# The last chunk's output projection in three PSUM banks (256, 256, 128 columns), stored as 512 and 128 columns

## Chip, cores, metric

The kernel runs on one core of a Trainium2 chip. The metric is the device time of one execution in microseconds (us); of repeated runs the median is quoted. "The profile" is one profiled execution; its span is the time from its first to its last instruction, here about 1.3 us shorter than the run's own time. Words used below: a bank is a piece of PSUM (`PS` in the code), the memory into which TensorE writes its sums; taking a bank out of it is an eviction; a store is issued by an instruction of a queue and lands when its completion is signalled; the tail is what follows TensorE's last matmul. In the profile's lines PE is TensorE, PEld its weight loads, DVE VectorE, ACT ScalarE, SPq and ACTq the queues of SyncE and ScalarE.

## The reference, cut to what matters

```python
g = sigmoid((x * gate_w).sum(-1, keepdims=True))
a = 2.0 * einsum("blp,dp->bld", hseq, Cmat).real + x * Dskip   # state space branch, hseq: a scan over L
b = gelu(x @ w1 + b1) @ w2 + b2                                # dense branch
return g * a + (1 - g) * b                                     # 2048 x 640, bfloat16
```

There are 2048 rows of 640 columns, taken as 16 chunks of 128 rows. What is changed is the last step of the last chunk: the product of the scanned state with `Cmat` (real and imaginary part, 5 blocks of 128 each, so 10 matmuls for each block of columns), times the gate, plus everything else.

## The kernel before

For every chunk `c`, `cproj(c)` multiplies the state `H` by `CT` into two PSUM banks. For all chunks but the last, ScalarE takes the banks out into `E2`, VectorE adds the three parts in two steps, and one store writes 128 x 640. For the last chunk the sum of the other parts is made ahead in `E2`, VectorE takes each bank out with one instruction (times gate, plus `E2`), and each part is stored as soon as it is there:

```python
CCOLS = (slice(0, D - 256), slice(D - 256, D))          # 384 and 256 columns

def cproj(c):
    for hf in range(2):
        bank = next_bank()
        cbank[hf] = bank
        cols = CCOLS[hf] if c == NCH - 1 else slice(hf * HALF, (hf + 1) * HALF)
        n = cols.stop - cols.start
        def f_mm(bank=bank, cols=cols, n=n):
            for ci in range(2):
                for k in range(KP):       # KP = 5
                    t = nc.tensor.matmul(PS[bank][:, 0:n], H[b % NHB][:, ci, k, s * 128:(s + 1) * 128],
                                         CT[:, ci, k, cols], start=(i == 0), stop=(i == 2 * KP - 1))
        # ... other chunks: ScalarE evicts to E2
def comb(c):
    # ...
    if c == NCH - 1:
        # "last": E2 = xg + E1
        for hf in range(2):
            cols = CCOLS[hf]
            def f_fin(...):   # VectorE: osb[:, cols] = PS * gcol + E2[:, cols]
            def f_st(...):    # SyncE:  o2[c * 128:(c + 1) * 128, cols] <- osb[:, cols]
        return
```

## Time and profile before

| | before |
|---|---|
| median of 3 runs | 213.53 us (213.41 to 214.03) |
| span of the profiled run | 212.3 us |
| TensorE busy | 99% |
| from TensorE's last matmul to the end of the span | 2.1 us |

First the page of the kernel before: the busy time of each engine (with its share and its number of instructions), and the chain of work that ended last.

```profile
PE 209.3 (99%) x1264; PEld 120.6 (57%) x1264; DVE 189.2 (89%) x262; ACT 111.3 (52%) x201; POOL 3.0 (1%) x11
...
PE 99%; DVE 0%; issue 0%
```

The chain is TensorE's from one end to the other. Its last pieces in order of time (start, length, what; kernel before):

```profile
204.69 5.45 PE ps L817 x40
210.13 0.03 issue
210.16 0.48 DVE osb L850
```

Line 817 is the projection; the 40 matmuls are those of the last two chunks. After them come one eviction and a store. The timeline of VectorE at the end (start, length, engine, line, operation, tiles; in brackets the idle time before it and what ended that):

```profile
208.00 0.49 DVE L480 TENSOR_TENSOR osb<-xg,E 128x640 bf16<-128x640 bf16 x1 [2.15 <-ACT E L828]
208.53 0.49 DVE L480 TENSOR_TENSOR osb<-osb,E 128x640 bf16<-128x640 bf16 x1
209.07 0.62 DVE L850 SCALAR_TENSOR_TENSOR osb<-ps,gcol,E 128x384 bf16<-128x384 f32 x1
210.16 0.48 DVE L850 SCALAR_TENSOR_TENSOR osb<-ps,gcol,E 128x256 bf16<-128x256 f32 x1 [0.47 <-PE ps L817]
```

VectorE is not the bound here: it sits idle for 0.47 us before the last eviction, until TensorE has filled the bank. The queue of SyncE, and the transfers by size with their median time from issue to landing:

```profile
209.04 0.33 SPq L870 DMA_DIRECT2D out_dram<-osb  x1
209.71 0.33 SPq L856 DMA_DIRECT2D out_dram<-osb  x1
210.67 0.33 SPq L856 DMA_DIRECT2D out_dram<-osb  x1
```

```profile
out_dram<-osb SPq DMA_DIRECT2D x1, 96.0 KB, 1.6
out_dram<-osb SPq DMA_DIRECT2D x1, 64.0 KB, 1.5
```

So what follows TensorE is 0.48 us of eviction and about 1.6 us of store. Apart from the ten matmuls that it adds, the change can act on nothing else.

### The profile page before, as it was taken

The page shows a single profiled execution, that of the slowest core. Times are in us where ns is not written, and L with a number is a line of the kernel's source. Part 1 is how long each engine was busy: PE and PEld are TensorE (multiplying, and loading weights), DVE is VectorE, ACT ScalarE, POOL GpSimd, SP SyncE. Part 2 cuts the span into 40 slices and gives each one's busy share as a digit, 9 for nine tenths or more (in the row PEclk, how much of TensorE's full clock was granted, in tenths as well). Part 3 has the DMA queues.
Part 4 walks back from the last instruction along what each step waited for, and adds up shares of the span by engine and source line. Part 5 has one row for each costly group of instructions (what it writes and reads, how often), then busy time and mean ns, then how long its engine had stood idle before and what let it go on. Part 6 is the DMA issues. An engine that isn't in the chain of part 4 may idle for free.

```text
span 212.3 us, 3122 instructions
## 1 busy us (share of the span) xinstructions
PE 209.3 (99%) x1264; PEld 120.6 (57%) x1264; DVE 189.2 (89%) x262; ACT 111.3 (52%) x201; POOL 3.0 (1%) x11
## 2 busy tenths in 40 slices
PE   8999999999999999999999999999999999999995
PEld 3444444444567776444466777444446777767773
DVE  2499999999999999999999969899999999899443
ACT  2489556678905234556953233556792444722330
POOL 2000000000000010000000001000000000000000
DMA  5999799997000004100000014000000000010011
GB/s 147 316 263 203 161 221 317 274 213 173 24 0 3 31 31 127 62 0 0 0 3 0 0 36 154 31 31 3 0 0 2 3 31 31 31 34 0 31 34 62
DMA packets 31318, 16.35 MB, mean 77 GB/s; under 512 B 22984, under 2 KB 30408, under 8 KB 31304
## 3 DMA queue, kind: packets, MB, share of 16 engines
q1 hardware_dynamic: 30928, 14.83, 27.4%
q0 software_dynamic: 320, 1.31, 2.0%
q8 instruction: 10, 0.16, 0.3%
q14 instruction: 4, 0.03, 0.1%
q10 hardware_dynamic: 56, 0.01, 0.0%
HBM read 7.63 MB, written 2.62 MB: 48 GB/s over the span
## 4 chain that ended last, share of the span: by engine, by line
PE 99%; DVE 0%; issue 0%
PE ps L769 27%; PE ps L639 22%; PE ps L817 20%; PE ps L682 20%; PE ps L619 4%; PE ps L399 1%; PE ps L783 1%; PE ps L660 1%; PE ps L411 0%; DVE osb L850 0%; PE ps L430 0%
## 5 line engine op out<-in xcount | busy, mean ns | idle before, releaser
L769 PE MATMUL ps<-W2sb,Gl 128*128 128x320 bf16 x416 | 59.2, 299 | 0.0
L769 PEld LDWEIGHTS ps<-W2sb,Gl 128*128 128x128 bf16 x416 | 40.4, 98 | 17.0 <-issue 1.1
L639 PE MATMUL ps<-xT,W1sb 128*128 128x512 bf16 x220 | 48.1, 379 | 0.0
L817 PE MATMUL ps<-CT,H 128*128 128x320 bf16 (+2 forms) x320 | 45.4, 299 | 0.0
L722 DVE TENSOR_TENSOR_SCAN W<-atab,V 128x1280 bf16<-128x1280 f32 x16 | 44.3, 2811 | 0.3
L682 PE MATMUL ps<-xT,BT 128*128 128x512 bf16 x200 | 43.8, 379 | 0.0
L817 PEld LDWEIGHTS ps<-CT,H 128*128 128x128 bf16 x320 | 31.3, 98 | 12.2
L797 ACT ACTIVATE E<-ps,g1col 128x320 bf16<-128x320 f32 x32 | 16.3, 527 | 39.7 <-PE ps L769 25.5
L639 PEld LDWEIGHTS ps<-xT,W1sb 128*128 128x128 bf16 x220 | 21.6, 98 | 25.9
L646 ACT ACTIVATE Gl<-ps,cols 128x512 bf16<-128x512 f32 x44 | 29.6, 689 | 10.0 <-PE ps L639 10.0
L682 PEld LDWEIGHTS ps<-xT,BT 128*128 128x128 bf16 x200 | 19.4, 98 | 23.5 <-ACT Gt L668 0.4
L691 ACT ACTIVATE U<-ps 128x512 bf16<-128x512 f32 x40 | 23.8, 597 | 14.9 <-PE ps L682 14.9
L828 ACT ACTIVATE E<-ps,gcol 128x320 bf16<-128x320 f32 x30 | 15.8, 527 | 22.6 <-PE ps L817 22.6
L756 ACT ACTIVATE ps<-b2b 128x320 f32<-128x320 bf16 x32 | 14.1, 442 | 1.1
L480 DVE TENSOR_TENSOR osb<-xg,E 128x640 bf16<-128x640 bf16 x15 | 7.3, 488 | 7.9 <-ACT E L828 7.5
L836 DVE SCALAR_TENSOR_TENSOR xg<-xn,gcol,dsk 128x640 bf16<-128x640 bf16 x16 | 13.9, 883 | 0.4
L596 DVE SCALAR_TENSOR_TENSOR scr<-xn,gwb 128x640 bf16<-128x640 bf16 x16 | 13.2, 823 | 0.4
L480 DVE TENSOR_TENSOR V<-V,W 128x1280 bf16<-128x1280 bf16 x16 | 12.5, 821 | 0.3
L480 DVE TENSOR_TENSOR H<-H,V 128x1280 bf16<-128x1280 bf16 x16 | 12.5, 821 | 0.3
L480 DVE TENSOR_TENSOR V<-mr,U 128x2560 bf16<-128x2560 bf16 x8 | 11.9, 1489 | 0.2
L480 DVE TENSOR_TENSOR H<-c,W 128x2560 bf16<-128x2560 bf16 x8 | 11.9, 1490 | 0.2
L480 DVE TENSOR_TENSOR V<-s,W 128x2560 bf16<-128x2560 bf16 x8 | 11.9, 1484 | 0.0
(80 smaller groups left out, 100.2 us busy)
## 6 DMA issues: line engine op xcount, KB each, us to landing
out_dram<-osb SPq DMA_DIRECT2D x15, 160.0 KB, 1.8
W2sb<-in_B_w_dram SPq DMA_DIRECT2D x1, 2080.0 KB, 9.2
W1sb<-in_B_w_dram SPq DMA_DIRECT2D x5, 256.0 KB, 4.8
xn<-in_A_x_dram POOLq DMA_DIRECT2D x2, 640.0 KB, 4.7
xn<-in_A_x_dram SPq DMA_DIRECT2D x1, 640.0 KB, 7.7
W1sb<-in_B_w_dram SPq DMA_DIRECT2D x1, 480.0 KB, 5.8
W1sb<-in_B_w_dram SPq DMA_DIRECT2D x1, 400.0 KB, 6.4
xn<-in_A_x_dram SPq DMA_DIRECT2D x1, 384.0 KB, 6.0
```

Of the source, the lines that this page charges most:

```text
L480: return inc("dve", nc.vector.tensor_tensor(out=o, in0=a, in1=b, op=o_))
L639: t = nc.tensor.matmul(PS[bank][:, :], W1sb[:, k, jf * 128:(jf + 1) * 128], xT[q][:, k, :], start=(k == 0), stop=(k == KD - 1))
L646: return inc("act", nc.scalar.activation(Gl[q % 2][:, jf, :], PS[bank][:, :], ACT.Gelu_apprx_tanh, bias=b1col[:, jf:jf + 1]))
L682: t = nc.tensor.matmul(PS[bank][:, :], BT[:, ci, kd, k * 128:(k + 1) * 128], xT[q][:, kd, :], start=(kd == 0), stop=(kd == KD - 1))
L691: return inc("act", nc.scalar.activation(dst, src, ACT.Copy, scale=1.0 if ci == 0 else -1.0))
L722: t = inc("dve", nc.vector.tensor_tensor_scan(out=g[:, ci, :], data0=a, data1=v[:, ci, :], initial=0.0, op0=ALU.mult, op1=ALU.add))
L756: return inc("act", nc.scalar.activation(PS[bank][:, 0:HALF], b2b[:, cols], ACT.Copy))
L769: t = nc.tensor.matmul(PS[bank][:, 0:HALF], Gl[q % 2][:, jf, t4 * 128:(t4 + 1) * 128], W2sb[:, jf, cols], start=False, stop=False, skip_gr ...
L797: return inc("act", nc.scalar.activation(E1[c % NE][:, cols], PS[bank][:, 0:HALF], ACT.Copy, scale=g1col[:, c:c + 1]))
L817: t = nc.tensor.matmul(PS[bank][:, 0:n], H[b % NHB][:, ci, k, s * 128:(s + 1) * 128], CT[:, ci, k, cols], start=(i == 0), stop=(i == 2 * K ...
L828: return inc("act", nc.scalar.activation(E2[c % NE][:, cols], PS[bank][:, 0:HALF], ACT.Copy, scale=gcol[:, c:c + 1]))
L836: return inc("dve", nc.vector.scalar_tensor_tensor(out=xg[c % 2][:, :], in0=xn[q % 2][:, c % 4, :], scalar=gcol[:, c:c + 1], in1=dsk[:, :] ...
```

## The change

The intent: what is done after the last matmul should be smaller. The last bank gets 128 columns in place of 256, so that its eviction and its store are shorter. The other 512 columns are cut in two banks, so that VectorE can take out the first while TensorE fills the second; both go out in one store. The price is ten more matmuls with their weight loads, one more eviction, and rows of 256 bytes in the last store. The cut-down diff:

```diff
-        CCOLS = (slice(0, D - 256), slice(D - 256, D))
+        CCOLS = (slice(0, 256), slice(256, D - 128), slice(D - 128, D))
+        SCOLS = (slice(0, D - 128), slice(D - 128, D))
 
         def cproj(c):
-            for hf in range(2):
+            for hf in range(len(CCOLS) if c == NCH - 1 else 2):
 ...
-                for hf in range(2):
-                    cols = CCOLS[hf]
+                for hf, cols in enumerate(CCOLS):
 ... one eviction (fin) for each bank, marking ("osbl", hf); it waits for the store of chunk c - NO, as before
+                for i, cols in enumerate(SCOLS):
+                    def f_st(i=i, cols=cols):
+                        return dma_inc("sp", nc.sync.dma_start(o2[c * 128:(c + 1) * 128, cols], osb[c % NO][:, cols]), f"stl{i}")
+                    op(f"stl{i}", "sp", 0.5, [("osbl", hf) for hf in ((0, 1), (2,))[i]], [], f_st, prio=1000 + c, lat=2.5)
```

More of the change, by code (lines that the diff above doesn't have):

```diff
@@ L830, in cproj @@
                 op(f"e2_{c}_{hf}", "act", d_act(HALF), [("bank", bank), ("g", q)], [("E2", c % NE, hf)], f_ev, prio=5)
+        stores = {}
         def comb(c):
@@ L851, in f_fin @@
                                                                         in1=E2[c % NE][:, cols], op0=ALU.mult, op1=ALU.add))
-                    op(f"fin{hf}", "dve", d_dve(HALF), [("bank", cbank[hf]), ("E2", c % NE, 0), ("E2", c % NE, 1)], [("osb", c % NO, hf)], f_fin, prio=-60)
-                    def f_st(hf=hf, cols=cols):
-                        return dma_inc("sp", nc.sync.dma_start(o2[c * 128:(c + 1) * 128, cols], osb[c % NO][:, cols]), f"stl{hf}")
-                    op(f"stl{hf}", "sp", 0.5, [("osb", c % NO, hf)], [], f_st, prio=1000 + c, lat=2.5)
+                    op(f"fin{hf}", "dve", d_dve(cols.stop - cols.start), [("bank", cbank[hf]), ("E2", c % NE, 0), ("E2", c % NE, 1)], [("osbl", hf)], f_fin,
+                       prio=-60, after=[stores[c - NO]])
+                for i, cols in enumerate(SCOLS):
+                    def f_st(i=i, cols=cols):
+                        return dma_inc("sp", nc.sync.dma_start(o2[c * 128:(c + 1) * 128, cols], osb[c % NO][:, cols]), f"stl{i}")
+                    op(f"stl{i}", "sp", 0.5, [("osbl", hf) for hf in ((0, 1), (2,))[i]], [], f_st, prio=1000 + c, lat=2.5)
                 return
@@ L870, in f_st @@
                 return dma_inc("sp", nc.sync.dma_start(o2[c * 128:(c + 1) * 128, :], osb[c % NO][:, :]), f"st{c % NO}")
-            op(f"st{c}", "sp", 0.5, [("osb", c % NO, 0), ("osb", c % NO, 1)], [], f_st, prio=1000 + c, lat=2.5)
+            stores[c] = op(f"st{c}", "sp", 0.5, [("osb", c % NO, 0), ("osb", c % NO, 1)], [], f_st, prio=1000 + c, lat=2.5)
         def outs(q, mid=None):
```

## The prediction

> **What bounds the kernel now.** The engine table gives TensorE 209.3 of 212.3 us (99%), VectorE 189.2, and the chain of waits is 99% TensorE. The change touches only what follows the last matmuls. The timeline of the last microseconds shows: the last chunk's projection starts at about 207.26; its 384-column bank needs 10 matmuls at about 163 ns, its 256-column bank 10 at about 109 ns. VectorE finishes chunk 14's combine at 209.02, evicts 384 columns at 209.07 (0.62 us), then idles 0.47 us for TensorE, and evicts 256 columns at 210.16 (0.48 us, to 210.64). The queue issues the stores at 209.71 and 210.67 (0.33 us of sequencer each); the tables of transfers give issue to landing 1.6 us (96 KB) and 1.5 us (64 KB). So the tail after the last matmul is 0.04 + 0.48 + 0.03 + 1.5 + about 0.1 = 2.2 us, 1% of the span. Nothing else can move.
>
> **What changes.** The projected columns stay 640. Ten matmul/weight-load pairs are added: 20 pairs become 30 (256, 256, 128 columns). One eviction is added, and the last becomes 128 columns. Two stores remain: 128 KB and 32 KB (256-byte rows instead of 512).
>
> - Matmuls: the trace's pace fits columns/2400 + 2.5 ns (136 ns at 320). If that holds at 128 columns (56 ns), TensorE ends about 0.02 us later. The Trainium skill, "TensorE: Matmul & The Clock Gate", section "Back-to-back issue gap", gives about 81 ns for a sustained weight-load/matmul stream at 128 columns; then it ends 0.27 us later. No warm 128-column stream is in this trace; the eight cold transposes at the start go at about 105 ns, equal to 128 columns at half clock, so loads hid there. I lean towards 60 to 75 ns: 0.05 to 0.2 us later. The last matmul itself drains 0.05 us sooner (219 ns against 272 for one of 256).
> - Evictions: two PSUM sizes give 1.05 ns per column (618 and 484), so 128 columns cost about 0.35 us (estimate), 0.13 less. VectorE: first 256 at 209.06 to 209.54; second when its bank is done, 209.63 to 210.11; the 128 can start at 210.15 at the earliest and, by TensorE, at 210.20 (56 ns) to 210.43 (81 ns). It ends at 210.55 to 210.78, before: 210.64.
> - Stores: the 128 KB store issues at about 210.14, landing about 1.7 us later (211.85), not last. The sequencer is free at 210.47. The 32 KB store issues at 210.58 to 210.81, before 210.67. Data start about 0.85 us after issue, when the 128 KB (about 0.5 us of movement) has just finished, so little collision. Landing falls only slightly from 1.5: 96 to 64 KB saved just 0.1 us. Risk: the skill's "DMA: Bandwidth & Descriptors", "Specifications", says that below 512 bytes the engine does a read-modify-write; no store in this trace shows it.
>
> All of it is on the critical path: eviction -0.13, drain -0.05, weight loads +0.02 to +0.27, landing -0.1 to +0.1. Sum about -0.25 to +0.2, centre -0.05 us.
>
> **Prediction:** 213.45 us, 8 in 10 within 213.1 to 213.85. Faster by over 2%: 0.5%; within 2%: 99%; slower: 0.5%.
>
> **What would show each step.** Timeline at the end: ten 128-column matmuls 56 to 81 ns apart; the last eviction about 0.35 us, starting 210.2 to 210.4; the larger store issued near 210.14, the smaller near 210.7; table of transfers: 32 KB landing 1.4 to 1.5 us. TensorE's start of the projection and everything earlier unchanged to 0.1 us.
>
> **What would make it wrong.** Weight loads at 98 ns each not hidden (+0.4 us); 256-byte rows landing slower; the two stores, now 0.5 us apart rather than 0.96, queueing on the same engines; a changed instruction order before the last chunk. Run-to-run spread (213.41 to 214.03) exceeds the effect.

## The result, and the profile after

| | before | after |
|---|---|---|
| median of 6 runs each | 213.47 us (213.16 to 214.03) | 213.49 us (213.26 to 213.88) |
| ratio | | 0.9999, 95% interval 0.9982 to 1.0015 |
| span of the profiled run | 212.3 us | 212.0 us |

A ratio here is the mean time of one kernel's fast runs over the mean of the other's of the same rounds, so it is not quite the ratio of the medians. The result is "the same". But the interval is 0.33% wide, 0.7 us, and the whole tail is 2.1 us. Whether the change did anything can only be seen in the trace. The lines of the kernel after that answer to those above, first the page:

```profile
PE 208.5 (98%) x1264; PEld 121.1 (57%) x1274; DVE 189.3 (89%) x263; ACT 111.3 (53%) x201; POOL 3.0 (1%) x11
...
PE 96%; DMA 2%; SPq 0%; issue 0%; DVE 0%
```

There are ten more weight loads and one more VectorE instruction. (There must be ten more matmuls too: ten matmul records of earlier stages, lines 619, 639 and 682, are missing from this trace.) The "DMA 2%" in the chain lies in the loading phase at the start, of which more below. The chain's last pieces, VectorE's timeline and the queue of the kernel after:

```profile
204.60 5.47 PE ps L818 x50
210.07 0.03 issue
210.10 0.35 DVE osb L852
```

```profile
208.85 0.48 DVE L852 SCALAR_TENSOR_TENSOR osb<-ps,gcol,E 128x256 bf16<-128x256 f32 x1
209.54 0.49 DVE L852 SCALAR_TENSOR_TENSOR osb<-ps,gcol,E 128x256 bf16<-128x256 f32 x1 [0.21 <-PE ps L818]
210.10 0.35 DVE L852 SCALAR_TENSOR_TENSOR osb<-ps,gcol,E 128x128 bf16<-128x128 f32 x1
```

```profile
210.05 0.33 SPq L861 DMA_DIRECT2D out_dram<-osb  x1
210.47 0.39 SPq L861 DMA_DIRECT2D out_dram<-osb  x1
```

```profile
out_dram<-osb SPq DMA_DIRECT2D x1, 128.0 KB, 1.7
out_dram<-osb SPq DMA_DIRECT2D x1, 32.0 KB, 1.5
```

Two traces must be lined up before such small times are compared: the two kernels reached the last projection at different moments (204.69 and 204.60 in the chain) though nothing before it was changed. So from here on, times count **from the first matmul of the last chunk's projection**, and are taken from the trace's records at 1 ns:

| us from the projection's start | before | after | difference |
|---|---|---|---|
| TensorE's last matmul ends | 2.881 | 2.905 | +0.024 |
| last eviction starts | 2.919 | 2.944 | |
| last eviction takes | 0.484 | 0.349 | -0.135 |
| last store's issue starts | 3.431 | 3.321 | |
| last store's issue takes | 0.332 | 0.387 | +0.055 |
| its first data move, after the issue's end | 0.501 | 0.513 | +0.012 |
| its data take | 0.348 | 0.265 | -0.083 |
| last data to end of span | 0.399 | 0.401 | +0.002 |
| **end of span** | **5.011** | **4.887** | **-0.124** |

The terms add up to the difference (within 1 ns of rounding). The matmuls and the narrower eviction behave as wanted. In the store, most of the 0.08 us that fewer bytes save is given back by a longer issue. That was to be explained.

### The profile page after: what moved, and what is told of

Same layout as the page of the kernel before. It is cut to its first block, busy times and chain, and to the rows that moved or that the text cites. A ratio compares the mean times of both kernels' runs of the same rounds, so it can differ in the third digit from the quotient of the medians.

```text
span 212.0 us, 3133 instructions
## 1 busy us (share of the span) xinstructions
PE 208.5 (98%) x1264; PEld 121.1 (57%) x1274; DVE 189.3 (89%) x263; ACT 111.3 (53%) x201; POOL 3.0 (1%) x11
## 4 chain that ended last, share of the span: by engine, by line
PE 96%; DMA 2%; SPq 0%; issue 0%; DVE 0%
PE ps L769 27%; PE ps L639 22%; PE ps L818 21%; PE ps L682 20%; PE ps L619 3%; DMA W1sb<-in_B_w_dram 2%; PE ps L783 1%; PE ps L660 1%; SPq L326 0%; DVE osb L852 0%; PE ps L430 0%
## 5 line engine op out<-in xcount | busy, mean ns | idle before, releaser
L639 PE MATMUL ps<-xT,W1sb 128*128 128x512 bf16 x215 | 47.5, 379 | 0.3
L682 PE MATMUL ps<-xT,BT 128*128 128x512 bf16 x196 | 43.1, 379 | 0.3 <-issue 0.2
L818 PEld LDWEIGHTS ps<-CT,H 128*128 128x128 bf16 x330 | 32.0, 98 | 11.7
```

The lines of the kernel that those rows point to most:

```text
L639: t = nc.tensor.matmul(PS[bank][:, :], W1sb[:, k, jf * 128:(jf + 1) * 128], xT[q][:, k, :], start=(k == 0), stop=(k == KD - 1))
L682: t = nc.tensor.matmul(PS[bank][:, :], BT[:, ci, kd, k * 128:(k + 1) * 128], xT[q][:, kd, :], start=(kd == 0), stop=(kd == KD - 1))
```

## The experiments

The theory: the change shortens the tail by a real 0.12 us, which is 0.06% and less than the noise of a run. The rivals: the difference of the traces is chance; only the narrow last eviction counts and the third bank is not needed; the split of the stores counts for nothing; or the 256-byte rows or the collision of the two stores eat up a larger gain. Each kernel below was timed in 5 rounds but for the last two, and all gave correct results. The edits are against the kernel after, unless said otherwise.

### 1. The kernel before, against itself

> The kernel before against itself: the noise of the comparison and the repeatability of the tail. All theories: same time, ratio 1.000 within its interval of about +-0.0015. In the profile: from the first matmul of the last chunk's projection to the end of the span 5.01 us within 0.03 (5.011 in the first trace), whatever the span does; from the start of the last store's issue to the end 1.58 us. If the first number scatters by more than 0.1 us, the 0.12 us that the first pair of traces shows for the change proves nothing.

Measured: the end comes 5.006 us after the projection's start (5.011 in the first trace), the last issue 1.576 us before the end. The time was 213.58 us against 213.72, ratio 0.9994, interval 0.9983 to 1.0006. So the tail repeats to 5 ns, while the timing of a kernel against itself is off by 0.06%, just the size that is sought.

### 2. The kernel after, again

> The changed kernel again. Theory 'small real gain, drowned': from the first matmul of the last projection to the end 4.89 us within 0.03 (4.887 in the first trace; before 5.011), and a measured ratio between 0.998 and 1.001, centred near 0.9994. Rival 'no gain at all, the first traces differed by chance': 5.0 us in the tail as before.

Measured: 4.879 us (4.887 in the first trace). The gain of 0.12 to 0.13 us in the tail is no chance. The time: 213.41 us against 213.72, ratio 0.9992, interval 0.9980 to 1.0003. This is no resolved gain either.

Where does the noise come from? The chain of waits in the first 20 us shows where it arises. These are single lines of the kernel before, of the kernel after, of the second run of the kernel after, and of the kernel of experiment 8 (`old_tail`):

```profile
14.09 5.40 PE ps L639 x25
```

```profile
14.00 5.40 PE ps L639 x25
```

```profile
14.64 5.39 PE ps L639 x25
```

```profile
13.74 5.40 PE ps L639 x25
```

Line 639 is the first layer's second part, the first matmuls after the load phase. Their start scatters by 0.9 us over these four traces. The last projection starts at 207.240, 207.154, 207.788 and 206.895 us in the same four: 193.15 us later each time, within 0.01 us. (The records at 1 ns say the same of all 13 traces of this document: from the first record of line 639 to the projection 193.315 to 193.318 us.) So nearly all of the scatter before the tail arises in the first 14 us. There the chain changes hands from run to run: in the second run of after it goes through the load of `xn`, in the first through a load of `W1sb`, in before through TensorE alone.

```profile
0.75 3.06 DMA xn<-in_A_x_dram
...
8.38 4.75 PE ps L619 x22
```

```profile
1.80 4.59 DMA W1sb<-in_B_w_dram
...
8.65 3.84 PE ps L619 x17
```

(The first fence is of the second run of after, the second of the first.)

The change of hands is not the cause by itself: in the second run of before the chain goes through `xn` too, and line 639 starts at 14.10 us, as in the first. The records of line 619, the matmuls before those of line 639, show what differs. They start 216 ns apart, but in some traces the first of them start about 427 ns apart, half the pace: before has two such slow steps, the second run of after four, the first run of after none. That second run starts line 639 0.55 us later than before does; of this, 0.10 us is a later start of line 619 (4.84 against 4.74 us) and 0.44 us the longer slow stretch. The first run of after instead loses 0.23 and 0.20 us in two stops of TensorE between these matmuls. Why the slow stretch is longer in one run than in another was not tested.

### 3. Two banks of 512 and 128: the store split alone

```diff
-CCOLS = (slice(0, 256), slice(256, D - 128), slice(D - 128, D))
+CCOLS = (slice(0, D - 128), slice(D - 128, D))
-((0, 1), (2,))[i]
+((0,), (1,))[i]
```

> The store split alone, with two banks of 512 and 128 columns. Theory: VectorE becomes the bound of the tail. The 512-column bank completes 2.36 us after the projection's start, its eviction takes about 0.75 us (estimate: 0.484 at 256 columns plus 1.05 ns for each further column), so the 128-column eviction starts at about 3.14 us after TensorE has been done 0.2 us, and the end comes 5.08 us after the projection's start: 0.2 us later than the changed kernel and 0.07 later than the kernel before. Rival 'only the width of the last eviction and the size of the last store count': 4.89 us, as the changed kernel.

Measured: the end at 5.12 us, 0.24 later than the kernel after and 0.11 later than the kernel before. (One matmul record of this projection is missing; the start was fixed by ScalarE's last eviction before it, which follows the start by 0.201 to 0.202 us in the other traces.) The time was 213.78 us, ratio 1.0004, interval 0.9991 to 1.0016. The rival is refuted by the tail: with 512 columns in the first bank, the third bank is needed. VectorE and the queue of this kernel:

```profile
209.51 0.75 DVE L852 SCALAR_TENSOR_TENSOR osb<-ps,gcol,E 128x512 bf16<-128x512 f32 x1 [0.58 <-PE ps L818]
210.18 0.34 DVE L852 SCALAR_TENSOR_TENSOR osb<-ps,gcol,E 128x128 bf16<-128x128 f32 x1
```

```profile
210.29 0.33 SPq L861 DMA_DIRECT2D out_dram<-osb  x1
210.66 0.43 SPq L861 DMA_DIRECT2D out_dram<-osb  x1
```

The 128-column eviction starts as soon as the 512-column one lets it, as the theory said, even 0.08 us before the other's recorded end (so it is done earlier than expected). But then the store queue holds it: the first issue is still running when the last eviction ends at 210.52, and the second takes 0.43 us. That part was not in the theory.

### 4. Three banks, one store of 640 columns

```diff
-SCOLS = (slice(0, D - 128), slice(D - 128, D))
+SCOLS = (slice(0, D),)
```

> Three banks as changed, but one store of 640 columns after the last eviction. Evictions unchanged: the last ends 3.29 us after the projection's start. Theory 'a store's landing grows with its bytes': 160 KB take 0.26 us longer to the last byte than 32 KB (1.42 against 1.17 us from issue in the traces so far), so the end comes at 5.14 us, and the gain of the change is lost twice over. Rival 'landing is a fixed cost and the split of the stores does nothing': 4.89 us.

Measured: the last eviction ends at 3.293 us, its store is issued at once, in 0.332 us, and the end comes at 5.141 us, where 5.14 was expected. The time was 213.71 us, ratio 0.9996, interval 0.9983 to 1.0009. The bytes of the last store count: without the split of the stores the three banks are worse than the kernel before.

### 5. One store for each bank

```diff
-SCOLS = (slice(0, D - 128), slice(D - 128, D))
+SCOLS = CCOLS                                       # 64, 64, 32 KB
-((0, 1), (2,))[i]
+((0,), (1,), (2,))[i]
```

> The changed kernel with one store per bank (64, 64, 32 KB). The last 32 KB store then follows 64 KB in place of 128 KB on the same engines. Theory 'the 32 KB store is a little delayed by the 128 KB store before it' (its data begin 0.90 us after issue, against 0.83 for the last store of the kernel before): data begin at 0.83 to 0.85 us and the end comes at 4.82 to 4.85 us after the projection's start. Rival 'the sequencer or descriptor generation is what delays it, by the number of stores': the end is at 4.89 us or later, and the issue of the last store takes 0.36 us or more again.

Measured: the end at 4.863 us, 0.02 earlier than after and between the two theories (4.82 to 4.85, and 4.89 or later). The last issue takes 0.385 us again, and its first data follow the issue's end by 0.498 us (0.505 and 0.513 in the two traces of after). So the collision with the 128 KB costs 0.01 to 0.02 us, and the stretch of the issue does not depend on the bytes of the store before it: it was another cause. The time was 213.40 us, ratio 0.9990, interval 0.9977 to 1.0002.

### 6. A last bank of 64 columns

```diff
-CCOLS = (slice(0, 256), slice(256, D - 128), slice(D - 128, D))
-SCOLS = (slice(0, D - 128), slice(D - 128, D))
+CCOLS = (slice(0, 256), slice(256, D - 64), slice(D - 64, D))
+SCOLS = (slice(0, D - 64), slice(D - 64, D))
```

> Banks of 256, 320 and 64 columns, stores of 576 and 64 columns. Rival 'the narrower the last eviction the better': 0.28 us in place of 0.35, end at 4.82 us after the projection's start. Theory 'VectorE queues': the 320-column bank completes at 2.66 us, its eviction takes 0.55 us to 3.21, the 64-column one ends at 3.51 and the end comes at about 5.08 us, 0.2 later than the changed kernel. And the pace of ten 64-column matmuls: 29 ns if columns/2400 + 2.5 ns still holds, about 56 ns if a weight load of 128 columns sets the floor.

Measured: the end at 5.182 us, 0.30 later than after. The time was 213.67 us, ratio 1.0009, interval 0.9995 to 1.0022. The evictions and the queue:

```profile
209.70 0.55 DVE L852 SCALAR_TENSOR_TENSOR osb<-ps,gcol,E 128x320 bf16<-128x320 f32 x1 [0.48 <-PE ps L818]
210.16 0.27 DVE L852 SCALAR_TENSOR_TENSOR osb<-ps,gcol,E 128x64 bf16<-128x64 f32 x1
```

```profile
210.27 0.33 SPq L861 DMA_DIRECT2D out_dram<-osb  x1
210.65 0.43 SPq L861 DMA_DIRECT2D out_dram<-osb  x1
```

The rival is refuted: a narrower last eviction made the tail longer. VectorE is again late with the middle bank, though by less than the theory said: the last eviction ends 3.39 us after the projection's start, where 3.51 was expected and where the kernel after has 3.29. The rest is added by the store queue: the last eviction ends at 210.44, but its store's issue starts at 210.65, behind the other, and takes 0.43 us.

The ten 64-column matmuls start 29 ns apart (28 to 30 by the records), so the weight loads (98 ns each by their records) hide even there, and the prediction's formula, columns/2.4 + 2.5 in ns (its text has the first term in us), holds from 64 to 512 columns.

### 7. The last store on ScalarE's queue

```diff
-return dma_inc("sp", nc.sync.dma_start(...), f"stl{i}")
+sq = ("sp", "act")[i]
+return dma_inc(sq, engines[sq].dma_start(...), f"stl{i}")
```

> The changed kernel with the last 32 KB store issued from ScalarE's queue, which is idle by then; everything else as changed. Theory 'its issue was held up behind the 128 KB store on the SyncE queue' (0.387 us against 0.333 for the others, data 0.07 us late): end at 4.82 to 4.84 us after the projection's start. Rival 'the 16 engines were still busy with the 128 KB': 4.87 to 4.89 us.

Measured: the end at 4.876 us, and the issue on the idle queue of ScalarE is stretched just as on SyncE's:

```profile
210.28 0.33 SPq L863 DMA_DIRECT2D out_dram<-osb  x1
210.70 0.38 ACTq L863 DMA_DIRECT2D out_dram<-osb  x1
```

So the queue of SyncE is not to blame, and a second queue gains nothing. The number agrees with the rival, but not its reason: experiment 5 has shown that the bytes in flight hardly count. The time was 213.53 us, ratio 0.9995, interval 0.9982 to 1.0008.

Across experiments 1 to 7, the stretch follows the distance between two issues. With starts about 0.375 us apart the second takes 0.43 us, 0.40 apart (the first two stores of experiment 5) 0.41, 0.42 to 0.43 apart 0.38 to 0.39, and 0.67 or more apart 0.33. Each stretched issue ends 0.80 to 0.81 us after the start of the one before it. The Trainium skill, "Perfetto Trace Analysis", section "DMA Instruction — HWDGE (DVE, Sync)", offers a candidate: the block that makes the descriptors is shared between two issuing sequencers and locked while it makes them, and the recorded length of an issue includes the wait for that lock. As it stands it does not fit: by the page the block is freed before the recorded end of an issue, but all the stretched issues above began 0.04 to 0.10 us after the recorded end of the one before. So the cause of the stretch stays open. Experiments 9 and 10 test its dependence on the distance, and the second queue once more.

### 8. The last chunk handled as all the others

```diff
-            for hf in range(len(CCOLS) if c == NCH - 1 else 2):
+            for hf in range(2):
-            if c == NCH - 1:       # in cproj and in comb
+            if False:
```

> The last chunk treated as all the others: two halves of 320 columns, evicted by ScalarE, combined by VectorE in two steps, one store of 160 KB. All theories agree on a long tail: last eviction by ScalarE 0.53 us, combine 1.0 us, store landing 1.8 us: about 6.4 us from the projection's start to the end, 1.4 us more than the kernel before. It calibrates the timing: if the tail counts one for one, the measured time is 1.4 us longer and the ratio 1.0064, clear of the interval. If part of the tail were hidden in the launch, the ratio would be smaller.

Measured: 6.343 us from the projection's start to the end, 1.33 us more than the kernel before; time 214.81 us against 213.50, ratio 1.0059, interval 1.0047 to 1.0072. The tail's 1.33 us over 213.5 us give 1.0062. The interval allows 1.0 to 1.54 us, so within its width the tail counts one for one in the measured time. A gain of 0.12 us there should then be one of about 0.12 us in the time (an estimate from this ratio); it is just too small to be timed.

### 9. Banks of 256, 224 and 160

```diff
-CCOLS = (slice(0, 256), slice(256, D - 128), slice(D - 128, D))
-SCOLS = (slice(0, D - 128), slice(D - 128, D))
+CCOLS = (slice(0, 256), slice(256, D - 160), slice(D - 160, D))
+SCOLS = (slice(0, D - 160), slice(D - 160, D))
```

> Banks of 256, 224 and 160 columns, stores of 480 and 160 columns. In the runs so far the second of two stores that were issued less than 0.45 us apart took 0.377 to 0.432 us of issue in place of 0.333, so that it ended 0.803 to 0.809 us after the first one's start. Here the first store goes out at about 2.73 us after the projection's start and the last at 3.35, 0.62 apart. Theory 'the second issue is stretched only while the first one's descriptors are being made': its issue takes 0.333 us, the last eviction is 0.03 us longer (0.38), the end comes at 4.87 us, equal to the changed kernel (4.88) or 0.02 better. Rival 'the second of two stores always takes longer': 0.38 us again and 4.92 us. Timed ratio to the kernel before: 0.9993, not resolved.

Measured: the issues are 0.62 us apart and both take 0.33 us.

```profile
210.06 0.33 SPq L861 DMA_DIRECT2D out_dram<-osb  x1
210.68 0.33 SPq L861 DMA_DIRECT2D out_dram<-osb  x1
```

The stretch is gone, and the last data come at 4.471 us (4.486 and 4.480 in after), although the eviction is 0.03 us longer and 40 KB move in place of 32. The end is at 4.897, because this time 0.43 us lay between last data and end, not 0.40 (no run shows why). So within 0.02 us it is equal to the kernel after: what the wider bank costs, the free issue pays. The time was 213.39 us against 213.58, ratio 0.9991, interval 0.9977 to 1.0006.

### 10. Both stores held until the last eviction is done, on one queue and on two (one look each)

```diff
-[("osbl", hf) for hf in ((0, 1), (2,))[i]]
+[("osbl", hf) for hf in range(3)]
```

The second kernel issues the 128-column store from ScalarE's queue as well, as in experiment 7.

> The changed kernel with both stores held until the last eviction is done (one queue). Theory 'two issues need about 0.806 us from the start of the first to the end of the second': the first starts at 3.32 us after the projection's start, the second ends at 4.13, its data begin 0.51 us later and the end comes at about 5.30 us, later even than one store of all 640 columns (5.14). Rival 'the store's bytes alone set its landing': the second would end at about 3.32 + 2 x 0.333 + 0.04 = 4.03 and the end come at 5.20.

> The same, but the 128-column store issued from ScalarE's queue, at the same moment as the other from SyncE's. Theory 'the resource that makes the descriptors is shared by both queues': the later of the two issues ends about 0.8 us after the start of the first (4.13 us), end at 5.25 to 5.30 us, no better than one queue. Rival 'each queue has its own': both issues take 0.333 us and end at 3.66, and the end comes at about 4.95 us, set by the 128 KB.

Measured on one queue: the second issue ends at 4.130 us and the end comes at 5.302 us, as the theory said.

```profile
210.79 0.33 SPq L861 DMA_DIRECT2D out_dram<-osb  x1
211.17 0.43 SPq L861 DMA_DIRECT2D out_dram<-osb  x1
```

On two queues:

```profile
210.96 0.33 SPq L863 DMA_DIRECT2D out_dram<-osb  x1
210.96 0.38 ACTq L863 DMA_DIRECT2D out_dram<-osb  x1
```

The end is at 5.292 us, within the theory's range and no better than one queue. But the recorded issues don't fit it: ScalarE's ends at 3.707 us, not at 4.13. What is late there are its data, whose first move 0.71 us after its issue's end in place of 0.50, 0.26 us after those of the other store. So two near-simultaneous stores do hinder each other whatever the queue, and a plain lock that is fully visible in the issue is too simple a picture of how. One rival is not excluded: in this run the data of the two stores overlap (4.15 to 4.72 us for the 128 KB, 4.42 to 4.81 for the 32 KB), so the engines that move the data may have held the smaller one. What exactly is shared stays open. (One run each, 214.08 and 214.24 us, state unknown, so the times say nothing.)

## Why the prediction was right, point by point

- **The time.** 213.45 us within 213.1 to 213.85 was predicted, 213.49 measured. This alone proves little: the range is far wider than the effect, and no change at all (213.47 before) would have been a hit too. Also right, and shown by the traces: all of the change lies in the tail and is less than the scatter of the runs. Experiment 8 shows that the tail counts in full within its interval, experiments 1 and 2 that the scatter before the tail arises in the first 14 us.
- **TensorE.** The text leaned towards 60 to 75 ns for a 128-column matmul, between the formula (56 ns) and the 81 ns of the Trainium skill, "TensorE: Matmul & The Clock Gate", section "Back-to-back issue gap". The trace has 56 ns: in the line of the kernel after below, six matmuls take 0.50 us, of which the last one's own 0.22, so five steps take 0.28. TensorE ended 0.024 us later. Here the page's figure does not hold.

```profile
209.50 0.50 PE L818 MATMUL ps<-CT,H 128*128 128x128 bf16 x6
```

- **The sum counted the drain twice.** The 0.02 us at 56 ns was already the shift of TensorE's end, which includes the shorter last matmul (0.219 in place of 0.272 us); "drain -0.05" was taken off once more. That the centre was not too optimistic for this is due to an error the other way, the pace: the middle of "+0.02 to +0.27" is +0.145, 0.12 above what was measured. That the two errors partly cancel is luck. The slow pace also explains two signs that missed: in the time of the first trace the last eviction was to start at 210.2 to 210.4 and the smaller store to be issued near 210.7; aligned with that trace they come at 210.18 and 210.56.
- **Eviction.** 0.35 us was predicted, 0.349 measured: -0.135 us. This is the gain.
- **Landing.** From issue to end 1.580 us became 1.566, inside the predicted -0.1 to +0.1, but as a sum of two terms: 0.083 less for the data, 0.055 more for the issue (and 0.012 before the first data). The text named "queueing on the same engines" as a risk for stores 0.5 us apart. The stores were 0.42 us apart and did hinder each other, but in the issue (0.055 us); the bytes still in flight cost 0.01 to 0.02 us (experiment 5).
- **Rows of 256 bytes.** The feared cost did not come: the data of 128 rows took 0.27 us at 256 bytes and 0.35 at 512, and 0.23 at 128 (experiment 6). There is no step.
- **The centre.** -0.05 us was predicted, -0.12 is in the traces, in a range of -0.25 to +0.2. The mis-sized terms were the pace of the matmuls ("+0.02 to +0.27" was +0.024) and the drain (-0.05, already in it).

## What to carry to other kernels

At the end of a kernel, what follows the last matmul counts in the time (here one for one, within the interval of experiment 8), but it is a small sum: size its pieces (eviction, issue, data, receipt) from the trace before cutting finer, and line two traces up at the first changed instruction, for the run-to-run scatter may come from the start of the kernel (here from how long its first matmuls ran at half pace, and from stops between them) and be larger than the gain. A smaller last piece pays only while the engine that takes out the piece before it, and the store before it, are out of the way: here the best sizes let TensorE, not VectorE, release the last eviction, and kept the last two store issues 0.42 to 0.62 us apart. A second issuing queue does not help where the stores are that close.

## What the Trainium skill lacked or had wrong

- "TensorE: Matmul & The Clock Gate", section "Back-to-back issue gap": it gives about 81 ns per matmul at 128 columns and about 131 at 512 for a stream of weight-load/matmul pairs, and says that the formula for the isolated gap misses. Here the formula was right: 56 ns at 128 columns, 29 at 64, 109 at 256, 162 at 384, and 216 at 512 (25 matmuls of line 639 in 5.40 us), each with its own weight load of 98 ns, hidden.
- "DMA: Bandwidth & Descriptors", section "Specifications": a read-modify-write is stated for less than 512 bytes. No run here shows a cost of it in stores of 128 rows: first to last data 0.23 us at 128 bytes a row, 0.27 at 256, 0.28 at 320, 0.35 at 512, 0.43 at 768, 0.52 at 1024, 0.59 at 1280.
- "Perfetto Trace Analysis", section "DMA Instruction — HWDGE (DVE, Sync)", describes the lock on the block that makes descriptors and frees it before the recorded end of an issue. Here an issue of 0.33 us was stretched to 0.38 to 0.43 when another store had been issued 0.43 to 0.37 us before, on the same queue or another, though the recorded issue of that other had ended 0.04 to 0.10 us before; no page gives such a stretch. With two queues at the same moment the stretch was 0.05 us only and the data came 0.2 us later (one run); the page does not foresee that.
- That a VectorE instruction may start before the one ahead has ended is told, but no page gives the size: here an eviction that was ready started, by its record, about 0.08 us before the recorded end of the instruction ahead of it (210.18 against 209.51 + 0.75 in experiment 3).
